# Loading q by two queues, with the small loads behind it and ScalarE's table load first

## The chip, the cores and the metric

The kernel runs on one core of one Trainium2 chip. The core has TensorE (PE, matrix products into PSUM), VectorE (DVE), ScalarE (ACT), GpSimd (POOL) and SyncE (SP), which here only issues transfers. ScalarE can issue transfers too, from its own queue. Both queues feed the same 16 DMA engines. The metric is the device time of one execution in microseconds (us); the median of several runs counts.

## What is computed

A block with two branches on an input q of 2048 rows (tokens) and 640 channels, modulated by a conditioning vector c. The first branch (H3) makes a short causal convolution of k over 4 taps, multiplies it by v, convolves the product with a filter as long as the sequence (by FFT in the reference), and gates it with the normalized input. The second (a token mixer) is a two-layer perceptron across the tokens.

```python
def _A_ref(q, k, v, shift_k, ssm_k, ssm_D):
    ...
    for t in range(ks):
        k_shift = k_shift + k_pad[:, t:t + S, :] * shift_k[:, ks - 1 - t][None, None, :]
    kv = k_shift * v
    ...
    y = y + kv * ssm_D[None, None, :]
    return q * y

mod = (_silu(c) @ w_mod).reshape(c.shape[0], 6, 1, -1)
sa, ca, ga, sb, cb, gb = (mod[:, 0], mod[:, 1], mod[:, 2], mod[:, 3], mod[:, 4], mod[:, 5])
h = _layernorm(x, axis=-1) * (1 + ca) + sa
x = x + ga * _A_ref(h, A_k, A_v, A_shift_k, A_ssm_k, A_ssm_D)
h = _layernorm(x, axis=-1) * (1 + cb) + sb
x = x + gb * _B_ref(h, B_w1, B_b1, B_w2, B_b2)
```

Here x is q, S = 2048, D = 640, and the hidden width of the perceptron is 1728.

## The kernel before

The long convolution is done as a two-step Fourier transform by matrix products, in five chunks of 128 channels. For each chunk:

- `kv_ops` (on VectorE for three of four groups of rows, on GpSimd for the third group, g = 2) makes the short convolution times v from the tiles KX and VX (tile `in`) and writes X (tile `x`). Each group has eight instructions of 128 x 512. They are recorded by the helper at line 59.
- `step1` (L216) is the first transform step, for kv (side 0, from X) and for the filter (side 1, from tile `p`, to which `perm`, L162, copied it). Each of its four calls a side ends in a copy out of PSUM by ScalarE (L218) into tile `z`.
- `f2` (L232) is the second step, in eight groups g. The constant tiles `w` (w2, two halves of 2 MB) hold its weights: groups 0 to 3 use the first half, 4 to 7 the second. Each group leaves one PSUM tile, of which ScalarE copies one half (L236, tile `kt`) and VectorE multiplies both (two instructions into tile `p`); GpSimd then adds pairs of products into tile `y`. PSUM tiles go round in a ring of three, so group g + 3 waits until the products of group g are done.
- `i2` (L261) and `i1` (L277) are the way back, and `gate` multiplies by the normalized q and adds.

The work stands in the order in which the code is written (a manual schedule): each engine takes its instructions in that order, and waits on semaphores set by the builder. While f2 of the first chunk runs, VectorE also does the last group of the second chunk's `kv_ops` (the list `fill`, one instruction a group of f2, the first of them ahead of the products of group 0). Then come the batch statistics of q (L528), the transpose of the small rows (L539), and the modulation rows (`mod_part`, L347, from w_mod loaded at L340); when `mod_part` has read its tiles, the next filter (L150) and the constant v (L547) are loaded into them.

Transfers: at the start the taps (`load_taps`, L146), k and v are loaded, the lower 64 partitions by SyncE and the upper 64 by ScalarE. After that all loads are SyncE's, in the order of the code: k and v of the second chunk (`kv_loads`) with the two halves of w2 between (L465, L467), six small loads of b1, b2 and c into the tile `g` (L469 to L472), the taps of the third chunk, and q in 16 loads of two rows a partition (L487), lower and upper partitions in turn, into the tiles `xa` (rows j = 0 to 7 of a partition) and `xb` (8 to 15). Behind q stand the loads of w_mod.

The builder gives every load one of eight semaphores, in turn over both queues, in the order in which it expects the loads to be issued. A load waits until the previous one on its semaphore has landed.

## Time and profile before

| what | us |
|---|---|
| median of 3 runs | 742.08 |
| the three runs | 743.94, 737.12, 742.08 |
| the profiled execution | 737.33 |
| its span | 735.5 |
| TensorE busy in it | 653.1 |
| VectorE busy in it | 499.4 |
| ScalarE busy in it | 299.5 |
| GpSimd busy in it | 176.2 |

The span goes from the first to the last instruction of the program; all times of views count from its start. The page of the profile gives busy time by engine and in 40 slices of 18.4 us. Two lines of the slices show the share of the span that the transfers take and what they moved:

```profile
DMA  9989988445420174950000535335163333555410
GB/s 180 241 235 255 265 228 167 97 80 132 89 61 4 29 198 151 187 116 2 0 1 21 95 77 96 58 59 110 55 186 101 92 117 110 153 164 172 145 55 36
```

Each digit is the busy share of the 16 DMA engines in tenths: the first seven slices, 130 us, are those in which transfers are dense. The change lies in the first four of them. The engine names have a q at the end (SPq, ACTq) where a queue's issuing is meant.

### The profile page before, as it was taken

How to read it: one execution, taken by the hardware profiler on the slowest of the kernel's cores; microseconds unless marked ns; L12 is line 12 of the kernel's file. 1: busy time of each engine (PE TensorE's matmuls, PEld its weight loads, DVE VectorE, ACT ScalarE, POOL GpSimd, SP SyncE). 2: the span in 40 equal slices, each digit the busy share in tenths (PEclk: the TensorE clock that was granted, in tenths of full speed). 3: DMA queues.
4: the chain of work that ended last, by engine and by line, in shares of the span. 5: the costliest groups of instructions: out<-in, count | busy, mean ns of one | idle time of the engine just before them, and what ended most of it. 6: DMA issues, size and time to landing. Idle time of an engine off the chain costs nothing.

```text
span 735.5 us, 20693 instructions
## 1 busy us (share of the span) xinstructions
PE 653.1 (89%) x9107; PEld 630.5 (86%) x9107; DVE 499.4 (68%) x857; ACT 299.5 (41%) x441; POOL 176.2 (24%) x176
## 2 busy tenths in 40 slices
PE   0797969999999989655899999999999989999997
PEld 0787749989989978544899999999999989999997
DVE  7756659969877548488994321231298958888886
ACT  0432465645646535425665512321235322333222
POOL 5197048626329047022440000000000000000000
PEclk9999889999999999657899999999999999999999
DMA  9989988445420174950000535335163333555410
GB/s 180 241 235 255 265 228 167 97 80 132 89 61 4 29 198 151 187 116 2 0 1 21 95 77 96 58 59 110 55 186 101 92 117 110 153 164 172 145 55 36
DMA packets 171921, 84.90 MB, mean 115 GB/s; under 512 B 88852, under 2 KB 165431, under 8 KB 171831
## 3 DMA queue, kind: packets, MB, share of 16 engines
q1 hardware_dynamic: 167282, 82.26, 45.5%
q10 hardware_dynamic: 4548, 1.31, 1.1%
q8 instruction: 71, 1.16, 0.7%
q14 instruction: 20, 0.16, 0.1%
HBM read 73.07 MB, written 10.49 MB: 114 GB/s over the span
## 4 chain that ended last, share of the span: by engine, by line
PE 58%; DVE 22%; issue 6%; DMA 4%; POOL 4%; ACT 3%; SPq 2%; ACTq 0%; DVEq 0%; POOLq 0%
PE pst L424 26%; PE pst L216 9%; PE pst L941 7%; PE pst L232 6%; DVE m_w L59 4%; PE pst L261 4%; POOL y L59 3%; PE pst L277 3%; DVE m_x L59 3%; DVE tap L59 3%; DVE kt L59 2%; ACT m_w L854 2%; PE pst L866 2%; DVE m_x L875 1%; DVE m_v L59 1%
## 5 line engine op out<-in xcount | busy, mean ns | idle before, releaser
L232 PE MATMUL pst<-z,w 128*64 128x64 f32 x2560 | 96.8, 241 | 11.7 <-ACT z L218 6.1
L232 PEld LDWEIGHTS pst<-z,w 128*64 128x64 f32 x2560 | 95.3, 142 | 13.6 <-ACT z L218 7.3
L424 PE MATMUL pst<-r_z,wb 128*128 128x320 f32 x504 | 82.9, 321 | 16.4 <-ACT r_z L685 11.3
L59 POOL TENSOR_TENSOR y<-p 128x256 f32<-128x256 f32 x72 | 90.4, 1304 | 26.8 <-DVE p L59 26.6
L424 PEld LDWEIGHTS pst<-r_z,wb 128*128 128x128 f32 x504 | 79.1, 198 | 18.3 <-ACT r_z L685 12.5
L59 DVE TENSOR_TENSOR p<-pst,kt 128x512 f32<-128x512 f32 x80 | 52.7, 690 | 28.5 <-ACT kt L236 19.3
L216 PE MATMUL pst<-v,x 128*64 128x128 f32 x640 | 46.0, 303 | 23.6 <-DVE x L59 23.6
L218 ACT ACTIVATE z<-pst 128x1024 f32<-128x1024 f32 x40 | 45.8, 1146 | 48.6 <-PE pst L216 28.4
L216 PEld LDWEIGHTS pst<-v,x 128*64 128x64 f32 x640 | 44.0, 221 | 24.2 <-POOL t L449 23.6
L424 PE MATMUL pst<-h_x,wb 128*128 128x320 f32 x336 | 51.1, 309 | 0.0
L424 PEld LDWEIGHTS pst<-h_x,wb 128*128 128x128 f32 x336 | 49.7, 188 | 0.0
L236 ACT ACTIVATE kt<-pst 128x512 f32<-128x512 f32 x40 | 25.2, 630 | 59.4 <-PE pst L232 38.8
L261 PEld LDWEIGHTS pst<-v,y 32*128 32x128 f32 x1280 | 42.6, 204 | 6.8 <-issue 2.6
L261 PE MATMUL pst<-v,y 32*128 32x64 f32 x1280 | 44.7, 291 | 4.2 <-DVE y L59 1.4
L746 ACT ACTIVATE pst<-pst,sm 128x640 f32<-128x640 f32 x14 | 10.7, 767 | 86.1 <-PE pst L424 86.1
L59 DVE TENSOR_TENSOR wb<-x,wb 128x1024 fp32r<-128x1024 f32 (+1 forms) x32 | 36.8, 1188 | 12.0 <-ACT wb L413 11.9
L866 PE MATMUL pst<-r_z,m_w 128*128 128x320 f32 x222 | 42.8, 312 | 1.9 <-DVE m_w L59 1.4
L216 PE MATMUL pst<-v,p 128*64 128x128 f32 x640 | 37.8, 274 | 2.4 <-issue 2.4
L854 ACT ACTIVATE m_w<-m_v 128x896 fp32r<-128x896 f32 x24 | 22.2, 950 | 42.4 <-DVE m_v L59 29.5
L424 PE MATMUL pst<-h_a,wb 128*128 128x320 f32 x252 | 38.8, 309 | 0.0
L424 PE MATMUL pst<-r_v,wb 128*128 128x320 f32 x252 | 38.8, 309 | 0.0
L216 PEld LDWEIGHTS pst<-v,p 128*64 128x64 f32 x640 | 35.2, 137 | 3.6 <-issue 3.2
(213 smaller groups left out, 1272.2 us busy)
## 6 DMA issues: line engine op xcount, KB each, us to landing
x<-in_B_w_dram SPq DMA_DIRECT2D x24, 512.0 KB
m_v<-in_B_w_dram SPq DMA_DIRECT2D x15, 384.0 KB
x<-in_B_w_dram SPq DMA_DIRECT2D x14, 384.0 KB
aux<-in_A_ssm_k_dram SPq DMA_DIRECT2D x10, 512.0 KB
in<-in_A_k_dram SPq DMA_DIRECT2D x36, 128.0 KB
in<-in_A_v_dram SPq DMA_DIRECT2D x36, 128.0 KB
m_x<-xs SPq DMA_DIRECT2D x28, 160.0 KB
out_dram<-m_x SPq DMA_DIRECT2D x28, 160.0 KB
```

The source lines that it names most:

```text
L59: TT = lambda eng, o, a, b, op: eng.tensor_tensor(o, a, b, op=op)
L216: pe.matmul(ps[64 * ri:64 * ri + 64, o:o + 128], lhs, F1[:, 128 * ri:128 * ri + 128], start=True, stop=True)
L218: evac = lambda: act.activation(Z[:, side, t].rearrange("p a k e -> p e a k"), ps.rearrange("p (e a k) -> p e a k", a=8, e=2), AF.Copy)
L232: pe.matmul(ps[64 * h:64 * h + 64, o:o + 64], W2[k1 // 32][:, 2 * (k1 % 32) + ri], rhs, start=True, stop=True)
L236: act.activation(kt.rearrange("p (m i) -> p m i", i=32), pv[:, :, 1], AF.Copy)
L261: pe.matmul(pp[qd // 2][:, o:o + 64], Y[p, ri, i:i + 2].rearrange("p i k -> p (i k)"), V2[p, 64 * ri:64 * ri + 64], start=ri == 0, stop=ri ...
L277: pe.matmul(ps[64 * b:64 * b + 64, 512 * e + 64 * jj:512 * e + 64 * jj + 64], V1[p, ri, n2], T2[p, :, 32 * ri + n2], start=ri == 0, stop=r ...
L424: pe.matmul(ps[0:m, h, 0:320], w_.bitcast(F32R), r_[:, 320 * h:320 * h + 320].bitcast(F32R), start=first and i == 0, stop=last and i == 2)
L746: act.activation(p, p, AF.Gelu_apprx_tanh, bias=B1C[:, f:f + 1])
L854: act.activation(W[n][0].bitcast(F32R), a(w_), AF.Copy)
L866: pe.matmul(bank[n], w[:, i].bitcast(F32R), r.bitcast(F32R), start=i == 0 and k == 0, stop=i == 6 and k == 2)
L941: pe.matmul(acc[s][:, h, 0:320], w[:, f_].bitcast(F32R), u[r + h].bitcast(F32R), start=f_ == 0 and k == 0, stop=f_ == NF - 1 and k == 2)
```

## The change

Three things are edited. ScalarE gets a copy of one column as its first instruction, with the loading of its function table ahead of it. The loads of q, 16 on SyncE, become two on ScalarE (upper 64 partitions, eight rows each) and four on SyncE (lower 64 partitions, four rows each), cut into runs of 2560 bytes instead of 5120. And the six small loads and the third chunk's taps move from ahead of the second chunk's work to behind q.

```diff
@@ -434,6 +434,7 @@
     dve.memset(epsc, EPS)
     for h in range(2):
         dve.memset(KX[64 * h:64 * h + 1, 0:3, :], 0.0)
+    act.activation(tm[:, 0:1], epsc, AF.Copy)
     both = (sync, act)
     load_taps(0, act)
     load_halo(0)
@@ -465,15 +466,9 @@
     sync.dma_start(T_w2[0], c_w2[:, 0:4096], max_dma_last_dim=4096)
     kv_loads(1, 3)
     sync.dma_start(T_w2[1], c_w2[:, 4096:8192], max_dma_last_dim=4096)
-    for h in range(2):
-        sync.dma_start(stg[7 * h:7 * h + 6, :], dram(b1, 864 * h, [[128, 6], [1, 128]]))
-        sync.dma_start(stg[7 * h + 6:7 * h + 7, :], dram(b1, 864 * h + 736, [[128, 1], [1, 128]]))
-    sync.dma_start(stg[14:30, :], dram(b2, 0, [[128, 16], [1, 128]]))
-    sync.dma_start(stg[30:35, :], dram(c, 0, [[128, 5], [1, 128]]))
     perm_add(0)
     perm(0)
     all_taps()
-    load_taps(2)
     for t in range(4):
         step1(0, t)
     run(kv_ops(2, pool))
@@ -482,10 +477,16 @@
     for t in range(4):
         step1(1, t)
 
-    for j in range(0, 16, 2):
-        for b in range(2):
-            sync.dma_start(XH[j // 8][64 * b:64 * b + 64, j % 8:j % 8 + 2],
-                           dram(q, (16 * b + j) * D, [[32 * D, 64], [D, 2], [1, D]]))
+    for b, n in ((1, 8), (0, 4)):
+        for j in range(0, 16, n):
+            both[b].dma_start(XH[j // 8][64 * b:64 * b + 64, j % 8:j % 8 + n],
+                              dram(q, (16 * b + j) * D, [[32 * D, 64], [D, n], [1, D]]), max_dma_last_dim=2560)
+    for h in range(2):
+        sync.dma_start(stg[7 * h:7 * h + 6, :], dram(b1, 864 * h, [[128, 6], [1, 128]]))
+        sync.dma_start(stg[7 * h + 6:7 * h + 7, :], dram(b1, 864 * h + 736, [[128, 1], [1, 128]]))
+    sync.dma_start(stg[14:30, :], dram(b2, 0, [[128, 16], [1, 128]]))
+    sync.dma_start(stg[30:35, :], dram(c, 0, [[128, 5], [1, 128]]))
+    load_taps(2)
 
     three = lambda t: [t[:, 640 * j:640 * j + 640] for j in range(3)]
     pl = [three(t) for t in (T_aux, T_aux[:, 2048:3968], T_v1, T_v1[:, 1920:3840], P)]
```

`both` is the pair (SyncE, ScalarE). The line numbers of the changed kernel are one higher from line 437 on; q's loads are L482 there, and the second half of w2 is L468. The names of PSUM tiles (pst and a number) differ by their numbers only.

## The prediction

> **What bounds the kernel now.** I read the chain of waits first, because the change only touches the first 100 us, and there the chain says which engine each stretch hangs on (start, length in us, what; "issue" is time in which the engine waited for nothing that the profile shows):

> ```profile
> 1.94 3.91 DMA in<-in_A_k_dram
> 6.08 0.71 DVE tap L59
> ...
> 22.81 0.70 DVE x L59
> ...
> 23.60 16.88 PE pst L216 x256
> 40.50 1.09 ACT z L218
> 41.63 13.09 PE pst L232 x345
> 54.72 1.28 issue
> 56.00 4.79 PE pst L232 x124
> 60.79 3.94 issue
> 64.73 2.00 PE pst L232 x36
> 66.72 9.21 PE pst L216 x123
> 75.95 1.08 ACT z L218
> 77.08 5.57 PE pst L261 x124
> 82.64 2.32 PE tap L347 x12
> 84.98 0.63 SPq L150
> ...
> 91.48 8.33 DMA v<-in_const_v_dram
> ```

> The chain starts with a ScalarE load of k, runs through VectorE's products without a gap, and is on TensorE from 23.60 to 84.96. The loads of q (L487) are not in it. What TensorE loses in step f2 (L232) is 1.28 + 3.94 = 5.22 us of "issue", inside runs of equal matmuls. Second, SyncE's queue in order of time (x is the number of loads), and the wait that stops it (us in total, times, longest):

> ```profile
> 32.50 4.39 SPq L130 DMA_DIRECT2D in<-in_A_k_dram  x2
> 36.93 0.72 SPq L467 DMA_DIRECT2D w<-in_const_w_dram  x1
> ...
> 39.81 6.48 SPq L146 DMA_DIRECT2D rows<-in_A_shift_k_dram  x2
> 46.34 5.07 SPq L487 DMA_DIRECT2D xa<-in_A_q_dram  x8
> 51.46 10.56 SPq L487 DMA_DIRECT2D xb<-in_A_q_dram  x8
> 62.99 1.85 SPq L340 DMA_DIRECT2D aux<-in_w_mod_dram  x2
> ```

> ```profile
> SPq L146 <- DMA w<-in_const_w_dram: 5.5, 1, 5.5
> ```

> The second tap load waits 5.5 us for the landing of the second half of the constant w2 (L467), although it has nothing to do with w2: every load counts up one of eight semaphores (DMAHW0 to 7) when it lands, the loads take these in turn, and a load is not issued before the one that had its semaphore before has landed. So q, queued behind, starts at 46.34. Third, the windows of 2 us (after the busy times: clock, DMA share, GB/s):

> ```profile
> 44.00:46.00 2.00, 2.00 (x61) 2.00 (x58) 1.07 (x2) 0.62 (x1) 1.92 (x2) 1.00 0.29 95
> 46.00:48.00 2.00, 2.00 (x61) 2.00 (x58) 1.53 (x4) 0.62 (x1) 1.84 (x3) 1.00 0.34 64
> ...
> 58.00:60.00 2.00, 2.00 (x63) 2.00 (x60) 1.54 (x4) 0.36 (x2) 2.00 (x2) 1.00 1.05 246
> ...
> 78.00:80.00 2.00, 2.00 (x60) 2.00 (x58) 1.93 (x7) 0.61 (x2) 0.00 (x0) 0.70 1.04 397
> ```

> The transfers idle at 44 to 48; then q, 64 partitions a load, moves at about 240 GB/s, and w_mod, 128 partitions a load, at 397, both at a DMA share of 1.0. This is the room that the change goes for. But since the chain never waits for q, filling it is worth nothing by itself; only a wait that is new, or the "issue" time, can move the end.

> **The change, part by part.** *The table load at the beginning.* ScalarE's first rows, before and now:

> ```order
> L989 UNCONDITIONAL_BRANCH [waits barrier_Pool_Activation_PE_DVE_SP_release]
> L146 DMA rows<-in_A_shift_k_dram 64x256 x2
> L130 DMA in<-in_A_k_dram 64x8x64 x2
> L130 DMA in<-in_A_k_dram 64x8x64 [waits DMAHW0_49]
> L130 DMA in<-in_A_k_dram 64x8x64 [waits DMAHW2_49]
> ```

> ```order
> L990 UNCONDITIONAL_BRANCH [waits barrier_Pool_Activation_PE_DVE_SP_release]
> L437 ACT_TABLE_LOAD
> L437 ACTIVATE sm<-sm 128x1 [waits DVE_49]
> L146 DMA rows<-in_A_shift_k_dram 64x256 x2
> L130 DMA in<-in_A_k_dram 64x8x64
> ```

> The table load and a one-column copy now stand ahead of ScalarE's first loads (taps, then k). The rows that price it:

> ```profile
> 0.71 1.20 ACTq L146 DMA_DIRECT2D rows<-in_A_shift_k_dram  x2
> ...
> 1.12 0.06 DVE L434 MEMSET sm<- 128x1 f32 x1
> ...
> 1.94 3.01 ACTq L130 DMA_DIRECT2D in<-in_A_k_dram  x4
> ...
> 21.81 1.28 ACT L162 ACT_TABLE_LOAD   x1 [21.81 <-DMA in<-in_A_k_dram]
> ...
> 23.10 2.12 ACT L162 ACTIVATE p<-aux 128x2048 f32<-128x2048 f32 x1
> ...
> 33.25 7.21 PE L216 MATMUL pst<-v,p 128*64 128x128 f32 x128
> ```

> Gain: the copy at 23.10 could start 1.28 earlier, but it ends at 25.22 and its reader starts at 33.25: nothing. Loss: ScalarE's loads, the head of the chain, start later, by at least 0.5 us (the copy needs the memset that ends at 1.18, against 0.71), at most 1.6 (1.28 for the table, some 0.3 for the copy). I take 1.2, nearer to the full table load, since before the copy at 23.10 started only when the table load had ended. VectorE runs from 6.08 to 23.5 without a gap, so all of it passes on. [...]

> *q on two queues.* ScalarE, around the new loads, before and after (pst are the PSUM results that it copies out):

> ```order
> L218 ACTIVATE z<-pst_316 128x2x512 [waits PE_49]
> L218 ACTIVATE z<-pst_334 128x2x512 [waits PE_49]
> L236 ACTIVATE kt<-pst_372 128x512 [waits PE_49]
> L236 ACTIVATE kt<-pst_407 128x512 [waits PE_49]
> L236 ACTIVATE kt<-pst_444 128x512 [waits DVE_49,PE_49,Activation_49]
> ```

> ```order
> L218 ACTIVATE z<-pst_309 128x2x512 [waits PE_49]
> L218 ACTIVATE z<-pst_327 128x2x512 [waits PE_49]
> L482 DMA xa<-in_A_q_dram 64x8x640 [waits DMAHW7_49]
> L482 DMA xb<-in_A_q_dram 64x8x640 [waits DMAHW2_49]
> L236 ACTIVATE kt<-pst_363 128x512 [waits PE_49]
> ```

> The two loads stand behind the eighth evacuation of step 1, which ends at 41.59 (chain), so they cannot be issued before. They cost ScalarE 2 x 0.75 (3.01 / 4) = 1.5 us, to 43.1. The next row on ScalarE starts at 44.28 (fence below): hidden. Now SyncE, from the last two k loads of the second channel chunk, before and after (w_75 is the second half of w2, g the small rows):

> ```order
> L130 DMA in<-in_A_k_dram 64x8x64 [waits DMAHW4_49]
> L130 DMA in<-in_A_k_dram 64x8x64 [waits DMAHW5_49]
> L467 DMA w_75<-in_const_w_dram 128x4x1024 [waits DMAHW6_49]
> L469 DMA g<-in_B_b_dram 6x128 [waits DMAHW7_49]
> L470 DMA g<-in_B_b_dram 1x128 [waits DMAHW0_49]
> L469 DMA g<-in_B_b_dram 6x128 [waits DMAHW1_49]
> ```

> ```order
> L130 DMA in<-in_A_k_dram 64x8x64 [waits DMAHW6_49]
> L130 DMA in<-in_A_k_dram 64x8x64 [waits DMAHW7_49]
> L468 DMA w_75<-in_const_w_dram 128x4x1024 [waits DMAHW0_49]
> L482 DMA xa<-in_A_q_dram 64x4x640 [waits DMAHW1_49]
> L482 DMA xa<-in_A_q_dram 64x4x640 [waits DMAHW2_49]
> L482 DMA xb<-in_A_q_dram 64x4x640 [waits DMAHW3_49]
> ```

> What moved is more than q. The semaphores go round over both queues, in the order in which the program's builder expects the issues, and it expects ScalarE's q loads early: in the built program the one of xa holds DMAHW7 just before the second L130 here, the one of xb DMAHW2 just before the second SyncE load of q. So SyncE's last k load now waits until ScalarE's q load has landed, and w2's second half is queued behind it. Before, both were issued by 37.65.

> The times: ScalarE issues xa at 41.6. Its 64 x 8 x 2560 B = 1.31 MB take 5.5 us at 240 GB/s, and a load has some 3.0 us beside its bytes (8.33 for the 2.10 MB of the constant v, of which 5.3 are bytes at 397 GB/s): landed at 50.2. k is then issued, 0.75; w2 at 50.9, and lands 8.3 later as v did, 1.0 more because the rest of ScalarE's xb moves beside it: 60.2. Ends: 58.1 (ScalarE's queue passes the last evacuation, 1.1, and no sharing, 1.0) and 62.5. Who waits:

> ```profile
> 40.05 0.69 DVE L59 TENSOR_TENSOR tap<-in,tap 128x512 f32<-128x512 f32 x1
> ...
> 44.28 0.62 ACT L236 ACTIVATE kt<-pst 128x512 f32<-128x512 f32 x1 [2.70 <-PE pst L232]
> ...
> 44.93 1.29 DVE L59 TENSOR_TENSOR p<-pst,kt 128x512 f32<-128x512 f32 x2 [4.18 <-ACT kt L236]
> ...
> 48.92 16.77 POOL L59 TENSOR_TENSOR y<-p 128x256 f32<-128x256 f32 x14
> ...
> 68.72 0.88 DVE L528 BATCH_NORM_STATS2 sm<-xa 128x6 f32<-128x320 f32 x2
> ```

> VectorE's product at 40.05 is the first of the last k group. It stands ahead of f2's products (44.93), so these wait for k: 50.2 + 3.9 (the landing of k at 1.94) = 54.1, and the first pair ends at 56.1. f2 has three PSUM buffers, so its fourth group starts then. Its fifth needs w2's second half: 60.2. Without stalls f2 takes (66.73 - 41.63 - 5.22) / 8 = 2.49 us a group, so before the fifth started at 51.6. Four groups end at 60.2 + 9.9 = 70.1. GpSimd's 16 sums (1.2 us each, 19 in all) from 55 on end at some 75, before i2, which needs them and started at 77.08.

> *The "issue" time.* Its size and places fit with fetching instructions behind data:

> ```profile
> q8 instruction: 71, 1.16, 0.7%
> ```

> That is 71 packets with 1.16 MB, 16 KB each, and both stalls fall where q streams, from 48 on, in runs of 5120 B. Now q's runs are 2560 B, and TensorE waits before the fifth group anyway, in which time a fetch can catch up. Ends: 0 and all 5.2; I take 1.0, near to none, for the second stall at half the run length or less. f2 then ends at 71.1 against 66.73: +4.4.

> *Small loads behind q, four SyncE loads of q.* SyncE's q follows w2: 2.62 MB at 240 GB/s is 10.9 us, landed at 72 or 73; the batch statistics (68.72 before, behind f2's last product, so some 73 now) take 16 us and read the last rows last: hidden. The small rows land before the transpose ahead of i2. The second tap load waits for the last q, so w_mod goes out at 73 instead of 62.99: 4 loads of 0.98 MB at 397 GB/s are 9.9, with 3.0 landed by 86, when i2's first half ends at 82.64 + 5.6 = 88.2. Covered by 2 us; if that goes, the fourth part of L347 waits.

> **Sum:** +1.2 (table) + 4.4 (f2) = +5.6. The profiled execution had a span of 735.5 us in 737.33, so 741.1 and 742.9. The median of the three runs shown is 742.08, 4.75 above it: 742.08 + 5.6 = 747.7, which is 0.75%.

> **Rivals.** *The stalls stay and w2 is late* (slower by more than 1%): "issue" 5.2 instead of 1.0 gives +9.8, with w2 at 62.5 +12.1: 751.9 to 754.2. It decides from +7.4 on. For it speaks that q, w2 and instructions still share the queues at 56 to 70; against it, the shorter runs and TensorE's own pause.

> *The wait for xa hides* (not slower): if ScalarE's q load landed before SyncE reaches the last k load, w2 would be out at 37.7, f2 would start its fifth group at 51.6, and shorter runs would take the 5.2 of "issue": +1.2 - 5.2 = -4.0, 738.1. To be more than 1% faster it would need 3.4 more from TensorE's clock or other stalls. Against it stands the order on ScalarE: the evacuation at 40.50 is ahead of the load.

> *The table load holds ScalarE longer than its row says* (slower, still within 1%): at twice its 1.28 the loads at the head start 2.6 later instead of 1.2, and all else as forecast it is +7.0: 749.1. Against it stand the two rows at 21.81 and 23.10. [...]

> **How the numbers follow.** A measurement of this kernel can tell about 1% (7.4 us) from no change. Forecast (+1.8 to +7.4, within 1%): 0.60. Stalls stay: 0.27, all slower. The wait hides: 0.08, half of it faster by over 1%. Longer table load: 0.05, within 1%. So faster 0.04, same 0.69, slower 0.27. The bounds give +5.6 - 0.7 - 2.1 - 1.0 = +1.8 and +5.6 + 0.4 + 2.3 + 4.2 = +12.5; the runs before lie from 5.0 below to 1.9 above their median, so I go some 3 us below the low end: 740.5 to 754.5.

> **What would show it.** In the profile after: ScalarE's first load at about 1.9 instead of 0.71, and VectorE's product train starting at about 7.3; SyncE waiting at L130 for xa until about 50, and L468 issued at about 51; TensorE waiting in L232 twice, for VectorE at the fourth group and for w at the fifth until about 60; less "issue" in L232. The forecast is wrong if L468 is still issued near 37, if TensorE has no wait for w, or if later stages take back the 5 us, which I expect nowhere, since all loads after 85 are issued only when TensorE's steps release them.

## The result, and the profile after

The changed kernel takes 752.28 us (median of 4 runs, 751.13 to 753.65); the kernel before, run beside it, 740.43 us (737.12 to 743.94). The ratio is 1.0159, with a 95% interval of 1.0123 to 1.0196: slower, by 11.8 us. The forecast was 747.7, in a range of 740.5 to 754.5. So the sign and the range held, the size did not: the loss is twice the +5.6 of the sum, and its size is that of the rival "the stalls stay and w2 is late" (751.9 to 754.2).

The profiled execution of the changed kernel is its slowest run (753.65, span 751.9), and that of before is one of its fastest, so that the two traces are compared stage by stage and not by their ends. The chain of waits of the changed kernel from the first transform step on (start, length in us, what):

```profile
24.19 17.40 PE pst L216 x256
41.61 0.01 ACT z L218
41.62 9.62 DMA xa<-in_A_q_dram
...
51.26 7.95 DMA in<-in_A_k_dram
...
59.33 0.69 DVE tap L59
60.02 1.20 DVE p L59 x2
61.23 0.14 issue
61.36 3.68 PE pst L232 x64
65.05 4.23 PE pst L232 x93
69.28 0.93 issue
70.21 4.83 PE pst L232 x124
75.03 3.38 issue
78.41 2.19 PE pst L232 x36
80.60 9.56 PE pst L216 x128
```

Before, the chain stayed on TensorE through this whole stretch, but for "issue" and one copy by ScalarE. Now it leaves TensorE at 41.61, goes over ScalarE's load of q (9.62), SyncE's last load of k (7.95) and VectorE's product that needs this k, and is back on TensorE only at 61.36. The next step 1 starts at 80.60 instead of 66.72. SyncE's queue in order of time, and the wait that stops it (us in total, times, longest):

```profile
34.03 17.82 SPq L130 DMA_DIRECT2D in<-in_A_k_dram  x2
51.90 0.63 SPq L468 DMA_DIRECT2D w<-in_const_w_dram  x1
52.57 6.45 SPq L482 DMA_DIRECT2D xa<-in_A_q_dram  x2
```

```profile
SPq L130 <- DMA xa<-in_A_q_dram: 14.2, 1, 14.2
...
SPq L486 <- DMA w<-in_const_w_dram: 3.4, 1, 3.4
```

The second k load waits 14.2 us for a q load, only because the two have a semaphore in common; w2's second half, behind it in the queue, goes out at 51.90 instead of 36.93. It has landed by 64.94, when the small load that waits for it (L486) is issued: at the same moment as f2's fourth group ends (61.36 + 3.68 = 65.04), so that the fifth group, the first to need it, does not wait. What TensorE and VectorE see of it, in order of time (in brackets the idle time before, and what ended it):

```profile
42.74 7.34 PE L232 MATMUL pst<-z,w 128*64 128x64 f32 x192 [1.17 <-ACT z L218]
...
59.33 0.69 DVE L59 TENSOR_TENSOR tap<-in,tap 128x512 f32<-128x512 f32 x1 [18.19 <-DMA in<-in_A_k_dram]
...
61.36 7.92 PE L232 MATMUL pst<-z,w 128*64 128x64 f32 x157 [11.28 <-DVE p L59]
```

192 matmuls are three groups of f2: they fill the three PSUM tiles, and TensorE then stands still for 11.28 us. It is the only wait for another engine or a load inside f2. The loss up to the end of f2 can be taken apart. Before, the fourth group would start at 41.63 + 3 x 2.49 = 49.1; now it starts at 61.36, 12.3 later, of which 1.1 is the later start of f2 (42.74 against 41.63) and 11.2 the wait. From there to the end of f2 are 80.60 - 61.36 = 19.2 us, of which 4.3 is "issue" (0.93 + 3.38); before, it was 66.72 - 49.1 = 17.6 with 5.2 of "issue". So "issue" gives 0.9 back, and the five groups themselves take 14.9 instead of 12.4, 2.5 more. That last part goes with TensorE's clock, in windows of 2 us (PE, weight loads, VectorE, ScalarE and GpSimd busy, then the granted clock, DMA share, GB/s):

```profile
52.00:54.00 2.00, 0.00 (x0) 0.00 (x0) 0.00 (x0) 0.00 (x0) 0.00 (x0) 0.83 1.03 193
54.00:56.00 2.00, 0.00 (x0) 0.00 (x0) 0.00 (x0) 0.00 (x0) 0.00 (x0) 0.50 1.05 193
...
60.00:62.00 2.00, 0.64 (x12) 0.67 (x14) 2.00 (x5) 0.60 (x1) 1.30 (x2) 0.50 1.01 406
62.00:64.00 2.00, 2.00 (x44) 2.00 (x42) 2.00 (x4) 0.00 (x0) 2.00 (x3) 0.50 1.06 328
64.00:66.00 2.00, 1.99 (x38) 1.83 (x37) 1.57 (x4) 0.60 (x1) 2.00 (x2) 0.50 1.06 197
66.00:68.00 2.00, 2.00 (x52) 2.00 (x50) 1.73 (x3) 0.00 (x0) 2.00 (x3) 0.76 1.09 207
```

While TensorE waits its granted clock falls to half (1.00 from 50 to 52, 0.50 from 54 on), and it stays there for some 5 us after the work is back: the fourth group, 64 matmuls, takes 3.68 us where 2.49 was usual, and the next 93 matmuls 4.23 instead of 3.62. The 36 after the second stall take 2.19 instead of 1.40, again at a clock of 0.50 (78 to 80). Together 1.1 + 11.2 - 0.9 + 2.5 = 13.9. Of this, 2.9 comes back by the modulation rows (L358, 106.08 against 95.12), where L261 and L347 run nearer to the full clock than before (1.00 from 90 to 100; before, 0.72 from 80 to 90). TensorE's wait ahead of the way back (L277) then grows from 2.96 to 5.05, so that L277 starts at 112.50 against 99.95, 12.55 later.

At the head, ScalarE's rows are these:

```profile
0.71 1.28 ACT L437 ACT_TABLE_LOAD   x1 [0.71 <-PEq L976]
...
1.22 1.21 ACTq L146 DMA_DIRECT2D rows<-in_A_shift_k_dram  x2
...
2.01 0.20 ACT L437 ACTIVATE sm<-sm 128x1 f32<-128x1 f32 x1
```

The first loads go out at 1.22, in the middle of the table load, and step 1 starts at 24.19 against 23.60: 0.6 later. Step 1 itself then takes 17.40 instead of 16.88 us; over the runs below it lies between 16.5 and 17.7, for a reason that is not known.

### The profile page after: what moved, and what is told of

Its sections match the earlier page's. It is cut to its first block, busy times and chain, and to the rows that moved or that the text cites. A ratio compares the mean times of both kernels' runs of the same rounds, so it can differ in the third digit from the quotient of the medians.

```text
span 751.9 us, 20681 instructions
## 1 busy us (share of the span) xinstructions
PE 657.5 (87%) x9107; PEld 635.7 (85%) x9107; DVE 498.6 (66%) x857; ACT 299.4 (40%) x442; POOL 175.3 (23%) x176
## 3 DMA queue, kind: packets, MB, share of 16 engines
q8 instruction: 71, 1.16, 0.7%
## 4 chain that ended last, share of the span: by engine, by line
PE 57%; DVE 20%; DMA 8%; issue 5%; POOL 4%; ACT 4%; SPq 2%; ACTq 0%; DVEq 0%; POOLq 0%
PE pst L424 26%; PE pst L216 9%; PE pst L942 7%; PE pst L232 6%; PE pst L261 4%; DVE m_w L59 4%; POOL y L59 4%; PE pst L277 3%; DVE m_x L59 3%; DVE tap L59 2%; PE pst L867 2%; DMA in<-in_A_k_dram 2%; DMA p<-in_B_w_dram 1%; ACT m_w L855 1%; DVE m_x L876 1%
## 5 line engine op out<-in xcount | busy, mean ns | idle before, releaser
L232 PE MATMUL pst<-z,w 128*64 128x64 f32 x2560 | 99.1, 244 | 21.9 <-DVE p L59 11.5
L232 PEld LDWEIGHTS pst<-z,w 128*64 128x64 f32 x2560 | 97.3, 146 | 24.0 <-issue 16.5
L59 POOL TENSOR_TENSOR y<-p 128x256 f32<-128x256 f32 x72 | 89.3, 1287 | 42.4 <-DVE p L59 42.0
L59 DVE TENSOR_TENSOR p<-pst,kt 128x512 f32<-128x512 f32 x80 | 52.2, 688 | 26.4 <-ACT kt L236 19.6
L216 PE MATMUL pst<-v,x 128*64 128x128 f32 x640 | 48.2, 315 | 24.2 <-DVE x L59 24.2
L218 ACT ACTIVATE z<-pst 128x1024 f32<-128x1024 f32 x40 | 45.7, 1141 | 57.4 <-PE pst L216 35.6
L216 PEld LDWEIGHTS pst<-v,x 128*64 128x64 f32 x640 | 46.2, 223 | 24.7 <-POOL t L450 24.2
L236 ACT ACTIVATE kt<-pst 128x512 f32<-128x512 f32 x40 | 25.1, 627 | 71.9 <-PE pst L232 38.7
L261 PEld LDWEIGHTS pst<-v,y 32*128 32x128 f32 x1280 | 42.3, 204 | 6.5 <-POOL y L59 2.6
L261 PE MATMUL pst<-v,y 32*128 32x64 f32 x1280 | 44.3, 291 | 3.7 <-DVE y L59 1.8
L59 DVE TENSOR_TENSOR wb<-x,wb 128x1024 fp32r<-128x1024 f32 (+1 forms) x32 | 36.9, 1189 | 11.6 <-ACT wb L413 11.5
L216 PE MATMUL pst<-v,p 128*64 128x128 f32 x640 | 38.7, 280 | 2.2 <-issue 2.2
L216 PEld LDWEIGHTS pst<-v,p 128*64 128x64 f32 x640 | 36.4, 141 | 3.2 <-issue 2.6
```

The source lines that it names most:

```text
L59: TT = lambda eng, o, a, b, op: eng.tensor_tensor(o, a, b, op=op)
L216: pe.matmul(ps[64 * ri:64 * ri + 64, o:o + 128], lhs, F1[:, 128 * ri:128 * ri + 128], start=True, stop=True)
L218: evac = lambda: act.activation(Z[:, side, t].rearrange("p a k e -> p e a k"), ps.rearrange("p (e a k) -> p e a k", a=8, e=2), AF.Copy)
L232: pe.matmul(ps[64 * h:64 * h + 64, o:o + 64], W2[k1 // 32][:, 2 * (k1 % 32) + ri], rhs, start=True, stop=True)
L236: act.activation(kt.rearrange("p (m i) -> p m i", i=32), pv[:, :, 1], AF.Copy)
L261: pe.matmul(pp[qd // 2][:, o:o + 64], Y[p, ri, i:i + 2].rearrange("p i k -> p (i k)"), V2[p, 64 * ri:64 * ri + 64], start=ri == 0, stop=ri ...
```

## The experiments

All ratios are to the kernel before, run beside each experiment on the same chip. They are not the quotients of two medians, which differ from them most for e10_w2first (1.0106) and e1_sync (1.0094), inside the interval both times. "Next step 1" is the step that follows f2.

| run | what it is | median, us | ratio (95%) | "issue" in f2, us | next step 1 starts, us |
|---|---|---|---|---|---|
| before | | 740.4 | 1 | 5.2 | 66.7 |
| after | | 752.28 | 1.0159 (1.0123 to 1.0196) | 4.3 | 80.6 |
| e1_sync | after, all q loads on SyncE | 747.56 | 1.0071 (1.0031 to 1.0111) | 10.9 | 73.9 |
| e2_late0 | after, ScalarE's q loads one group later | 742.07 | 1.0028 (0.9989 to 1.0068) | 8.3 | 73.5 |
| e3_table | before + table load first | 739.43 | 0.9996 (0.9968 to 1.0024) | 5.4 | 67.9 |
| e5_runs | after, runs of 5120 B | 751.62 | 1.0150 (1.0105 to 1.0195) | 4.8 | 80.6 |
| e10_w2first | after, only k behind the wait | 748.10 | 1.0141 (1.0083 to 1.0199) | 2.1 | 78.0 |
| e11_w2only | after, only w2 behind the wait | 754.15 | 1.0179 (1.0135 to 1.0224) | 4.1 | 80.0 |
| e4_small | before + small loads behind q | 742.38 | 1.0012 (0.9981 to 1.0043) | 6.4 | 71.2 |
| e6_modfirst | before, w_mod ahead of q | 740.27 | 0.9994 (0.9957 to 1.0031) | 1.0 | 63.3 |
| e9_modw2 | before, w_mod ahead of the small loads and q | 740.98 | 1.0000 (0.9970 to 1.0031) | 1.0 | 63.0 |
| e8_split | before, w_mod between q's halves | 742.89 | 1.0037 (1.0005 to 1.0069) | 4.1 | 65.2 |
| e12_q128 | before, q to 128 partitions a load | 821.77 | 1.1117 (1.1061 to 1.1174) | 0 | 63.2 |
| e13_q8 | before, q to 8 partitions a load | 767.4 to 786.9 | none formed | 0 | 63.3 |

The theory behind e1, e2, e3 and e5: the wait of SyncE for ScalarE's q load carries most of the loss; rivals are q's own stream, the table load and the length of the runs.

**All of q on SyncE** (e1_sync). With no load on ScalarE's queue, SyncE has nothing to wait for there.

```diff
-            both[b].dma_start(XH[j // 8][64 * b:64 * b + 64, j % 8:j % 8 + n],
+            sync.dma_start(XH[j // 8][64 * b:64 * b + 64, j % 8:j % 8 + n],
```

> All six loads of q on SyncE, everything else as changed. Theory (SyncE's k and w2 wait on a semaphore for ScalarE's q load): w2's second half goes out near 37.5 us, no wait of SyncE for xa at the last k load, f2 of the first chunk ends at 65 to 69 instead of 80.6; time against before 0.995 to 1.003. Rival (the shorter runs of 2560 bytes, or the small loads behind q, cost the time): still 1.008 or more. Rival (the table load at the head): still 1.008 or more.

Measured: 1.0071 (1.0031 to 1.0111). w2's second half is issued at 38.49, and the wait for k is gone, but f2 now loses more to "issue" than ever. The chain of this run in f2:

```profile
50.37 2.17 issue
...
52.54 4.71 PE pst L232 x123
57.25 4.76 issue
...
62.01 5.76 PE pst L232 x121
67.78 3.97 issue
```

10.9 us in three stalls, where before had two of 5.2 together. The ratio lies above the theory's 1.003, and f2 ends at 73.9 instead of at 65 to 69: a miss. About half of the loss goes with the wait: by the ratios (1.0159 to 1.0071) 6.5 us, which is uncertain by some 4; in the trace L277 starts at 106.38, 6.1 earlier than in the changed kernel. A second cost stood behind it: q that streams over all of f2, to 72.

**ScalarE's q loads behind its copy of the first f2 group** (e2_late0), so that the builder gives them later semaphores, which neither the last k load nor w2 uses next; SyncE's q loads stay as in the changed kernel.

```diff
-    for b, n in ((1, 8), (0, 4)):
+    def load_q(eng, b, n):
...
+    load_q(sync, 0, 4)
...
+            if c == 0 and g == 0:
+                load_q(act, 1, 8)
```

> ScalarE's two q loads stand behind its copy of f2's first group, so that the builder gives them semaphores which no k load and not w2 use next; still two queues, same bytes and runs. Theory (the wait, not the two queues): w2 out near 37.5, ScalarE's q issued near 46, both halves of q move side by side at more than 300 GB/s, f2 ends at 65 to 69; time against before 0.990 to 1.003. Rival (two queues at once slow each other or starve k): q no faster than 240 GB/s in sum, f2 still ends after 73, time 1.008 or more.

Measured: 1.0028 (0.9989 to 1.0068), not told from the kernel before. Moving the two loads 3.8 us later on ScalarE (41.62 to 45.46) takes back some 9.7 us of the 11.8 by the ratios (0.0131 of 740, each ratio uncertain by some 3 us); in the trace, L277 starts 5.0 later than before instead of 12.55, which makes it 7.5. Both queues carry q as in the change, so two queues are not the harm; the wait ahead of k and w2 is. The wait itself has only moved: SyncE's last q load now stands 23.5 us behind ScalarE's, in the loads issued from 39.53 to 64.25, and nothing in f2 waits for that q. The ratio is the theory's, but f2's end is not: it comes at 73.5, with q at some 200 GB/s for most of the time, as the rival had it. The "issue" time is 8.3 here, so the two costs are again seen apart.

**The table load alone** (e3_table).

```diff
+    act.activation(tm[:, 0:1], epsc, AF.Copy)
```

> The kernel before with the table load and the one-column copy at the head alone. Theory: ScalarE's first load goes out at 1.22 instead of 0.71 and the rest is 0.5 to 0.6 us later: 1.000 to 1.002. Rival (the table load carries the loss): 1.007 or more.

Measured: 0.9996 (0.9968 to 1.0024). Step 1 starts at 24.18, 0.6 later, and nothing of it is left at the end that this can tell.

**Runs of 5120 bytes** (e5_runs): the changed kernel with q's runs as they were.

```diff
-                              dram(q, (16 * b + j) * D, [[32 * D, 64], [D, n], [1, D]]), max_dma_last_dim=2560)
+                              dram(q, (16 * b + j) * D, [[32 * D, 64], [D, n], [1, D]]), max_dma_last_dim=5120)
```

> The changed kernel with q in runs of 5120 bytes, as before, on two queues. Theory (the wait): still slower than before, 1.010 to 1.016, since the wait is there; xa lands 1 to 2 us earlier if the shorter runs are what lowered the rate from about 240 to 195 GB/s. Rival (the short runs are the cause of the loss): 1.005 or less.

Measured: 1.0150 (1.0105 to 1.0195), 0.66 us under the median of the changed kernel, inside both intervals; ScalarE's first q load lands after 9.25 us instead of 9.62, where 1 to 2 us were expected, and "issue" is 4.8. The length of the runs does nothing that this shows.

Next, which of the two loads behind the wait costs: the last k, or w2.

**Only k behind the wait** (e10_w2first).

```diff
-    kv_loads(1, 3)
     sync.dma_start(T_w2[1], c_w2[:, 4096:8192], max_dma_last_dim=4096)
+    kv_loads(1, 3)
```

> The kernel after with the second half of w2 queued on SyncE ahead of the last group's v and k, so that only the last k loads stand behind the wait for ScalarE's q load. Theory: late k alone costs about as much as both, because VectorE's products of f2's first groups stand behind the product that needs k: k lands near 59, f2's fourth group starts near 61, f2 ends at 77 to 81 (80.6 after), ratio to the kernel before 1.011 to 1.016. Rival: w2 is what costs; then the fifth group no longer waits, f2 ends at 71 to 75, ratio 1.003 to 1.008.

Measured: 1.0141 (1.0083 to 1.0199). The two last k loads are issued from 51.28 on, and the second, at 51.92, lands 7.55 us later; the chain of this run is as that of the changed kernel up to f2's fourth group, and TensorE again goes from the fourth to the fifth without a halt. Only the second of the two stalls is gone:

```profile
51.92 7.55 DMA in<-in_A_k_dram
...
61.59 7.71 PE pst L232 x155
69.30 2.09 issue
```

The next step 1 starts at 78.0, 2.6 earlier than in the changed kernel. So late k alone keeps most of the loss in f2 (11.3 of 13.9 us).

**Only w2 behind the wait** (e11_w2only).

```diff
+    load_q(1, 8, 0, 8)
+    load_q(0, 4, 0, 16)
...
+            if c == 0 and g == 2:
+                load_q(1, 8, 8, 16)
```

> The kernel after with ScalarE's second q load (xb) issued behind its copy of f2's third group; the semaphores then fall so that the last k loads wait for nothing and only the second half of w2 waits for ScalarE's load of xa. Theory: w2 is issued near 51 and lands at 58 to 65; f2's first four groups run through by 52 or so, the fifth starts at 58 to 65, four groups of 2.5 us and 1 to 4 us of issue time follow: f2 ends at 70 to 77, ratio to the kernel before 1.004 to 1.012. Rival: late w2 costs nothing of its own, since k sets the end: f2 ends near 67 to 70, ratio 1.000 to 1.003.

Measured: 1.0179 (1.0135 to 1.0224): above the expected 1.004 to 1.012. The fourth group is in time here, but w2's second half, issued at 50.10, needs 15.37 us, and TensorE stands for 12.85. ScalarE's second q load, issued at 49.44, moves beside it: from 54 to 60, by the transfer records, SyncE's queue moves 0.94 MB and ScalarE's 0.64.

```profile
50.10 15.37 DMA w<-in_const_w_dram
...
65.61 9.21 PE pst L232 x210
74.81 3.28 issue
```

So late k alone brings most of the loss, and late w2 alone all of it: the two waits lie beside each other and do not add. To mend one of them would have mended little.

Then "issue": what holds TensorE back in f2? The times at which the instruction packets (queue q8, 16 KB each) start in the traces, in us from the span's start. They come from the transfer records, not from a view:

```text
before       33.06 38.73 45.09 53.29 61.99 70.57 76.99
after        34.18 39.13 51.99 67.25 75.70 82.30
e1_sync      33.57 38.15 49.62 59.17 68.79 73.76
e2_late0     34.11 42.58 51.94 61.55 69.30 73.10
e4_small     33.46 39.28 50.79 59.68 67.06 71.89
e6_modfirst  33.23 38.86 45.59 50.43 57.67 66.21 74.76
e9_modw2     33.27 41.03 48.18 53.66 58.06 66.17 74.90
e12_q128     33.25 37.74 45.31 49.57 54.18 58.98 68.20
```

Each of the 16 stalls of f2 in these eight traces ends 2.3 to 3.0 us after such a packet starts: the two of before at 56.00 and 64.73, after packets at 53.29 and 61.99. Between two stalls lie 127 matmuls (rows x127) and as many weight loads: one packet is a block of about 128 of each, which f2 uses up in 4.8 us (70.21 4.83 above). In the kernel before, the blocks come 8.2, 8.7 and 8.6 us apart while q streams (45.09 to 70.57). With hardly anything moving they come 4.2 to 4.8 us apart (e12 from 45.31 to 58.98, at 53 GB/s from 48 on, and e6 from 45.59 to 50.43, where w_mod is issued only at 48.72). With w_mod streaming at some 400 GB/s they lie between: 7.2 us (e6, 50.43 to 57.67) and 5.5 (e9, 48.18 to 53.66). 8.7 - 4.8 = 3.9 is the second stall of before (3.94).

**The small loads behind q, alone** (e4_small): the part of the change that brings q forward.

```diff
-    for h in range(2):
-        sync.dma_start(stg[7 * h:7 * h + 6, :], dram(b1, 864 * h, [[128, 6], [1, 128]]))
...
-    load_taps(2)
...
+    for h in range(2):
+        sync.dma_start(stg[7 * h:7 * h + 6, :], dram(b1, 864 * h, [[128, 6], [1, 128]]))
...
+    load_taps(2)
```

> The kernel before with only one edit of the change: the six small loads and the third chunk's taps stand behind q; q keeps its 16 loads, lower and upper partitions in turn. Theory: q then starts near 38 us instead of 46 and streams over all of f2 (41.6 to about 67), so that the instruction blocks of f2 come late three times instead of twice: issue time in f2 of 6 to 11 us instead of 5.2, f2 ends at 68 to 73, ratio 1.002 to 1.008. Rival: only q read from one half of the partitions holds instructions back, alternating halves do not more than before: issue time near 5 us or less, f2 ends near 66.7, ratio 0.998 to 1.001.

Measured: 1.0012 (0.9981 to 1.0043); three stalls, 3.04 + 2.02 + 1.31 = 6.4 us, and f2 ends 4.5 us later than before. The stage after it runs at the full clock here (1.00 from 70 to 90), where before it was at 0.72 (80 to 90), and the way back starts only 0.7 later. f2's numbers are the theory's, the ratio does not tell it from the rival.

**w_mod ahead of q** (e6_modfirst).

```diff
+    for kk in range(4):
+        mod_load(0, kk, (T_aux[:, 0:1920], T_aux[:, 2048:3968], T_v1[:, 0:1920], T_v1[:, 1920:3840])[kk])
...
-    for kk in range(4):
-        mod_load(0, kk, (T_aux[:, 0:1920], T_aux[:, 2048:3968], T_v1[:, 0:1920], T_v1[:, 1920:3840])[kk])
```

> The kernel before with the four loads of w_mod ahead of q. Theory (what holds the instruction blocks back is a stream of loads to 64 partitions): w_mod, 128 partitions a load at about 400 GB/s, goes out at 46 and is through by about 58; fewer blocks fall into q; issue time in f2 of 0 to 4 us instead of 5.2, f2 ends at 62 to 66, ratio 0.993 to 0.999 if the batch statistics, which then get q some 10 us later (70 to 72), stay hidden. Rival 1 (any dense stream holds them back): issue time near 5 us again, ratio 0.999 to 1.002. Rival 2: the batch statistics wait for q and hold i2 or the gate back: ratio from 1.003 up.

Measured: 0.9994 (0.9957 to 1.0031). f2 runs as the theory has it, but the gain does not last, and the ratio is rival 1's. TensorE in order of time, and the window in which w_mod streams:

```profile
41.52 17.73 PE L232 MATMUL pst<-z,w 128*64 128x64 f32 x476 [1.17 <-ACT z L218]
60.23 1.53 PE L232 MATMUL pst<-z,w 128*64 128x64 f32 x36 [0.97 <-issue]
63.26 8.40 PE L216 MATMUL pst<-v,x 128*64 128x128 f32 x128 [1.50 <-DVE x L59]
...
77.61 2.41 PE L261 MATMUL pst<-v,y 32*128 32x64 f32 x40 [1.62 <-issue]
```

```profile
52.00:60.00 8.00, 7.26 (x198) 7.11 (x193) 6.00 (x10) 1.91 (x3) 8.00 (x7) 1.00 1.03 402
```

Two blocks came before w_mod filled the transfers; the one under w_mod is late by 0.97, and under q, from 60 on, they are 8.5 us apart again; the stall then stands in L261. So a dense stream of w_mod holds the blocks back too, but by less than q. And f2's end is no longer the bound: step 1 waits 1.50 for VectorE's x, so that 66.7 could at best become 63.3. By 101.74, when L277 starts (99.95 before), all is given back: it waits for the constant v, which SyncE issues at 93.09 instead of 91.48.

**w_mod ahead of the small loads too** (e9_modw2), with the same lines placed behind w2's second half and ahead of the small loads; `perm` and the taps move ahead with them:

```diff
     sync.dma_start(T_w2[1], c_w2[:, 4096:8192], max_dma_last_dim=4096)
+    perm_add(0)
+    perm(0)
+    all_taps()
+    for kk in range(4):
+        mod_load(0, kk, (T_aux[:, 0:1920], T_aux[:, 2048:3968], T_v1[:, 0:1920], T_v1[:, 1920:3840])[kk])
```

> The kernel before with w_mod right behind the second half of w2, ahead of the small loads, the taps and q. Theory of the 64-partition stream: w_mod fills the queues from 43 to about 54, of which the transfers stood idle at 44 to 48; q starts near 50 and lies over the end of f2 and the start of the next step 1; issue time in f2 of 1 to 4 us instead of 5.2; f2 ends at 63 to 66, and the following step 1 may lose 1 to 3 us instead; ratio 0.993 to 1.000. Rival (q too late for the batch statistics): ratio from 1.003 up.

Measured: 1.0000 (0.9970 to 1.0031). The next step 1 starts at 63.0; L261 then loses 2.49 to "issue". L277 starts at 98.81, 1.1 earlier than before, and nothing of that is left in the ratio.

**w_mod between the two halves of q** (e8_split): the loop over xa, the four loads of w_mod, the loop over xb.

```diff
-    for j in range(0, 16, 2):
+    for j in range(0, 8, 2):
...
+    for j in range(8, 16, 2):
+        for b in range(2):
```

> The kernel before with w_mod between the two halves of q (xa, then w_mod, then xb). Theory of the 64-partition stream: the first late block (under xa) stays, the second falls into w_mod at about 400 GB/s: issue time 2 to 4 us instead of 5.2, ratio 0.996 to 0.999. Rival (any dense stream): issue time near 5 us, ratio 0.999 to 1.002.

Measured: 1.0037 (1.0005 to 1.0069), a miss, since 0.996 to 0.999 was expected: "issue" is 0.73 + 3.40 in f2, since the second late block still falls under xa, and 2.38 more in L261 under xb.

**q to all 128 partitions in a load** (e12_q128).

```diff
-        for b in range(2):
-            sync.dma_start(XH[j // 8][64 * b:64 * b + 64, j % 8:j % 8 + 2],
-                           dram(q, (16 * b + j) * D, [[32 * D, 64], [D, 2], [1, D]]))
+        sync.dma_start(XH[j // 8][:, j % 8:j % 8 + 2],
+                       dram(q, j * D, [[16 * D, 2], [32 * D, 64], [D, 2], [1, D]]))
```

> The kernel before with q in eight loads of two rows to all 128 partitions instead of 16 to 64; all else as before. Theory (64 partitions a load are what makes q slow and holds the instruction blocks back): q moves at 350 to 400 GB/s and is through 7 to 9 us earlier; issue time in f2 0 to 3 us instead of 5.2; f2 ends at 62 to 65; ratio 0.990 to 0.998. Rival 1 (it is the queue's depth of data, not the partitions): issue time near 5 us, ratio 0.999 to 1.002. Rival 2: q at 400 GB/s, but the gain in f2 is given back in the next step, as with w_mod ahead of q: ratio 0.998 to 1.002 with f2 ending near 63.

Measured: 1.1117 (1.1061 to 1.1174). None of the three cases: q became slow, 53 GB/s at a DMA share of 0.14, 12.3 us a load, and held all behind it. But f2 with next to no stream beside it runs without a stall. Its window, and TensorE's rows:

```profile
48.00:60.00 12.00, 12.00 (x332) 12.00 (x330) 7.79 (x13) 3.17 (x5) 12.00 (x10) 1.00 0.14 53
```

```profile
41.32 19.05 PE L232 MATMUL pst<-z,w 128*64 128x64 f32 x512 [1.18 <-ACT z L218]
63.21 8.40 PE L216 MATMUL pst<-v,x 128*64 128x128 f32 x128 [2.84 <-DVE x L59]
```

All 512 matmuls in 19.05 us at the full clock, against 25.1 before; and again the next step waits for VectorE's x, until 63.2. A share of 0.14 is 2.2 of the 16 engines busy on average. The outermost size of q's source is 2 here, and 8 in the next run, where the share is 0.52, or 8.3 engines; that the size sets the share is an estimate from these two runs.

**q in loads of 8 partitions** (e13_q8).

```diff
-    for j in range(0, 16, 2):
-        for b in range(2):
...
+    for j in range(0, 16, 8):
+        for i in range(0, 64, 8):
+            for b in range(2):
+                sync.dma_start(XH[j // 8][64 * b + i:64 * b + i + 8],
+                               dram(q, (32 * i + 16 * b + j) * D, [[32 * D, 8], [D, 8], [1, D]]))
```

> The kernel before with q in 32 loads of eight partitions and eight rows each (lower and upper partitions in turn) instead of 16 loads of 64 partitions and two rows. It asks whether a q that does not occupy all of the transfer engines lets the instruction blocks of f2 pass: q that came by two partition groups a load (the run before) took a DMA share of 0.1 and left f2 without a stall, but was far too slow. Theory: a load of eight partitions occupies half of the engines; DMA share 0.5 to 0.7 while q moves at 150 to 240 GB/s, issue time in f2 0 to 2 us instead of 5.2, f2 ends at 62 to 64, and, as no dense stream follows in i2, the gain stays: ratio 0.990 to 0.997. Rival 1: the loads are spread over all engines again, DMA share 1.0 and issue time near 5 us: 0.999 to 1.002. Rival 2: q becomes slow (below 100 GB/s) and holds SyncE's queue, w_mod and the batch statistics behind it: ratio above 1.02.

Measured: 767.36 to 786.89 us in 5 runs, against 736.06 to 743.56 before: rival 2, slower by at least 23.8 us. The first half of the theory held in the trace: a DMA share of 0.52, and f2's 512 matmuls in 19.07 us without a stall. But q moves at 80 GB/s only, and the stalls are back in the next two steps, with 1.24 us in L216 and 2.76 in L261.

No version beats the kernel before by more than its interval.

## Why the prediction came out as it did

*The wait was right, the path behind it only in part.* The semaphore that the builder gives in turn over both queues made SyncE's last k load wait for ScalarE's q load: forecast until 50.2, measured 51.24; w2 issued at 50.9, measured 51.90; TensorE stopped before the fourth group. e2_late0 shows that this wait carries most of the loss, 7.5 to 9.7 us; by e1_sync it is some 6. But the sum went over w2, with the fifth group held until 60.2, and the prediction named a TensorE without a wait for w as a sign that it is wrong. That sign is there: w2 landed as the fourth group ended. What set f2's end was k, through VectorE's product: e10_w2first, in which w2 is early, keeps 11.3 of the 13.9 us.

*Where the sum went wrong.* f2 ends at 80.60, 9.5 later than the 71.1 of the sum. The fifth group starts at 65.05 instead of 60.2, 4.9 later. "Issue" takes 4.3 instead of 1.0, 3.3 more. The last four groups take 11.25 instead of 9.9, 1.3 more.

*The range held by luck.* f2's end came 13.9 later than before, more than the +12.5 of the upper bounds. The time stayed under 754.5 because later stages gave some 2 us back, which the prediction expected nowhere (13.9 in the trace, 11.8 by the medians), and because the median of before came out at 740.43 instead of 742.08. Luck too is that ScalarE's q load went out at 41.6, as forecast: it was to wait for the end of the eighth evacuation, and that came at 42.69. The load went out as the evacuation began, at 41.61.

*Step one that failed: when k lands.* The prediction took 3.9 us from its issue to its landing, the time of the first k load of the program, and so 54.1. It took 7.95, to 59.21. ScalarE's second q load was ahead of it: from 52 to 58, while k was under way, ScalarE's queue (q10) moved most of the bytes (queue, packets, MB, share of 16 engines):

```profile
q10 hardware_dynamic: 336, 0.82, 73.4%
q1 hardware_dynamic: 579, 0.34, 34.9%
```

This is the largest error, 5.1 us on the path, of which 1.0 is the later landing of xa.

*Step two: when w2 lands.* 8.3 us and 1.0 for the sharing were forecast, 60.2; measured some 13 us, 64.94. It cost nothing of its own here, since k was as late. The same cause: at 193 to 212 GB/s ScalarE's 2.6 MB of q, in the queue since 41.6, is through only near 57. The prediction put q at 240 GB/s, the rate of the 16 loads that went to lower and upper partitions in turn; each half by itself moves at some 200 (193 to 212 in the windows of this run from 46 to 58).

*Step three: "issue".* 1.0 was forecast, by shorter runs and TensorE's pause; measured 4.3. e5_runs takes the first reason away: run length does nothing. The second held only for the block that fell into the pause (51.99). What "issue" hangs on is the stream beside f2, that of q above all: as blocks came every 8.5 us and f2 uses one each 4.8, a block under q can cost TensorE some 3.7 us; the stalls measured 0.7 (e8_split) to 4.8 (e1_sync). That the fetch of instructions stands behind it, as the prediction supposed, is borne out by the stalls, each of which ends 2.3 to 3.0 us after a packet starts, by e12_q128, where the blocks come 4.3 to 4.8 us apart and f2 has no stall, and by e13_q8, where it has none either.

*A cost that the prediction did not have:* the clock at half after the pauses (0.50 in the windows from 60 to 66 and from 78 to 80), 2.5 us in f2.

*The table load* was taken at +1.2; it was +0.6 at the head (near the lower end, 0.5), and nothing measurable in e3_table. The step that failed is the assumption that ScalarE's loads wait for the table load to end: they went out at 1.22, while it ran to 1.99. The longer table load of the rival is not seen: 1.28, and ScalarE's copy began 0.02 after it.

*The small loads behind q* were costed at nothing, and alone they cost nothing that can be told (e4_small, 1.0012, 0.9981 to 1.0043), though by another account than the one given: f2 lost 4.5 us more, and got it back in the next stage from TensorE's clock.

*The rival whose size came about* was given 0.27. Of its two terms one was there, the "issue" (4.3 of 5.2); TensorE did not wait for w2. What argued against it, shorter runs and the pause, was no measurement; what argued for it, that q, w2 and instructions share the DMA engines from 56 to 70, stood in the trace. Where a sum needs several favourable terms at once, each from a row of another place, the case in which one fails deserves more.

What stays open: how the DMA engines choose between the queues, and why instructions come at the pace they do under q. In the kernel before, some 236 GB/s x 8.6 us = 2.0 MB move between two blocks; with one half at a time in e1_sync some 200 x 9.6 = 1.9 MB. That would fit a fixed amount of data ahead of each fetch, but under w_mod it is more (2.2 MB in e9, 2.7 in e6); this was not tested. And no run has q ahead of k on the DMA engines without the semaphore in common, so the two parts of k's delay, 14.2 us of wait and 4 us of slower transfer, are read from the trace of the changed kernel alone.

## What to carry to other kernels

When loads go to a second queue, look in the built program at which semaphore each gets, and which later load of the other queue gets the same one: here a long load held back a load of k, and w2 behind it, for 14.2 us. Time a load by what already stands in front of it on the DMA engines, on either queue, and not by the same load at a quiet place: the last k load took 7.95 us, the first of the program 3.91 in the kernel before. And idle bandwidth is no gain by itself: a denser stream beside long runs of small matmuls held TensorE's instructions back here (0.7 to 4.8 us a block under q), and an earlier end of one stage was taken up by the next wait.

## What the runs showed of the hardware that was not expected

In e2_late0 the loads on one queue waited for what the other already had under way. ScalarE's two q loads are issued at 45.46 and 46.13; in the window from 44 to 52 only SyncE's queue (q1) and one instruction packet move, and ScalarE's (q10) comes in the next window. Of the two answers, first 44 to 52, then 52 to 64 (queue, packets, MB, share of 16 engines):

```profile
q1 hardware_dynamic: 701, 1.79, 106.7%
q8 instruction: 1, 0.02, 1.1%
```

```profile
q10 hardware_dynamic: 852, 2.14, 88.6%
q1 hardware_dynamic: 206, 0.48, 16.6%
```

They did not wait to the end: by the transfer records both queues move from 53 to 56 in this run, and from 54 to 60 in e11_w2only (0.94 and 0.64 MB). While the lower half of q on one queue and the upper on the other moved at once, from 53.2 to 55.6, the rate was 256 to 333 GB/s, where one half alone has some 200.
